# The first two batches loaded by halves of their heads, and a new order of the first steps

## The chip, the cores and the metric

One core of one Trainium2 chip runs one launch of the program. The metric is device time in microseconds (us), the median of the runs shown; the profile comes from one more execution.

## The reference: what is computed

Four batches of 8 heads, 576 positions and 64 columns go through linear attention; its output, as 2304 rows of 512, goes through a mixture of four experts and then through a gated unit:

```python
q_s = exp(q - max(q, axis=-1));  q_s /= sum(q_s, axis=-1) + 1e-9      # softmax over the 64 columns
k_s = exp(k - max(k, axis=2));   k_s /= sum(k_s, axis=2) + 1e-9       # softmax over the 576 positions
kv  = einsum('bhsd,bhde->...', k_s, v)       # 64 x 64 for each head
x   = (q_s @ kv) as [2304, 512]
p   = domain_probs / (domain_probs.sum(-1) + 1e-9)
y   = sum over e of p[:, e] * (relu(x @ w1[e]) @ w2[e])               # 4 experts, 512 -> 1024 -> 512
g   = y @ w_gate;  val = y @ w_val;  out = (silu(g) * val) @ w_out    # 512 -> 1536 -> 512
```

All numbers are float32 (the three weights of the last unit are stored as 64-bit numbers and are decoded on the chip).

## The kernel before, in words

**Precision and products.** Each float32 operand of a matmul is split in a high part (a cast, on ScalarE) and a low part (the difference, on VectorE or GpSimd; both in `split`, L103-105), and each product is made of three matmuls (`mm3`, L107-111). Big products are made with seven products in place of eight, for which sums and differences of the blocks of x and of the weights are needed. `combine_x` (L372-388) makes those of x: four sums (L381-384), and the high and low parts of the seven terms; `combine_acc` (L392) calls it for the tokens that lie in SBUF. The tokens are taken in two halves of two batches; each half is cut in two parts, X and Y, and each part in two groups j of the 512 columns.

**Attention.** A batch has four groups g of two heads. `att_kv` (in the chains below: K) takes the maxima of k over the positions: VectorE's first maxima m (L194), transposes on TensorE (ktp, L198-199), a reduction mx (L202), and a matmul that broadcasts it (kmb, L205); then VectorE's subtraction e (L210, the last 64 positions L213), ScalarE's exponential (L216, L217), the kv product of five matmuls on TensorE (kvp, L221 and L225), and its scaling kk by the reciprocal of the sums rs (L234-239). `att_q` (Q) takes the maxima of q over the columns (L254, L255), subtracts them (L257, L258), takes exponentials (L261, L262), sums (L276, L277), reciprocals (L282, L283) and scales by them on GpSimd (L284, L285); one group of batch 0 takes its sums with the exponentials (qs). `att_x` (X) transposes q on TensorE (qtp, L303, L307), splits it (qT) and multiplies it with kk into x, which ScalarE copies out (L322, L324).

**The first steps.** The first two batches are loaded by `load_batch` (L884-917), all on SyncE's queue: batch 0's k lands in `acc[X]` (acc_67 in the order below), its q in `acc[Y]` (acc_68), v in the tiles vb_82 (heads 0 to 3) and vb_83 (heads 4 to 7); the last 64 positions of k, q and v lie in `rest` (rest_84). Batch 1 lies in the tiles called stage. The work on the two batches, on the first two units of weights and on the first two steps of the experts is cut in pieces by Python generators, and a string of names (L997) says in which order the pieces are written: K01 is the next piece of group 1 of batch 0's k, Q and X likewise (X010: batch 0, group 1, half 0), L and l load weights, A, B, O and o prepare them, P the probabilities, N and M finish x, C0 and C1 combine X's two groups, D0 and D1 Y's, S is a piece of the experts' steps. From that string a scheduler decides what stands on each engine; an engine works its row off in order and waits for semaphores of the others. From the third step on, the order is written out and the change does not touch it.

Of the kernel before, what the change touches and what calls it, by code (L numbers as in the profile page):

```python
# [27 lines left out]
def attention_experts_swiglu(ctx: ExitStack, tc: tile.TileContext, q, k, v, probs, w1, w2, wg, wv, wo, out):  # L28
# [12 lines left out]
    nc = tc.nc  # L41
    B, H, S, D = q.shape
# [329 lines left out]
    def combine_x(b, j, x0, x1, eng):  # L372


        n = N[b]
        h, l = xh[b][:, :, j, :], xl[b][:, :, j, :]
        x0, x1 = (x.rearrange("p (s n) -> p s n", s=2) for x in (x0, x1))
        low = nc.gpsimd
        split(h[:, 0], l[:, 0], x0[:, 0], low)
        split(h[:, 1:3], l[:, 1:3], x1, nc.vector)  # L380
        eng.tensor_tensor(x0[:, 1], x0[:, 1], x0[:, 0], ALU.subtract)  # L381
        eng.tensor_tensor(x1[:, 1], x1[:, 1], x0[:, 1], ALU.subtract)
        eng.tensor_tensor(x0[:, 0], x1[:, 1], x0[:, 0], ALU.subtract)
        eng.tensor_tensor(x1[:, 0], x1[:, 0], x1[:, 1], ALU.subtract)
        yield
        split(h[:, 3:5], l[:, 3:5], x0, low)
        split(h[:, 5:7], l[:, 5:7], x1, nc.vector)
        yield

    parts = {}  # L390

    def combine_acc(b, j, eng=None):  # L392
        if (b, j) not in parts:
            parts[b, j] = combine_x(b, j, accT[b][:, 2 * j, :], accT[b][:, 2 * j + 1, :], eng or nc.vector)
            next(parts[b, j])
        else:
            next(parts.pop((b, j)))
# [386 lines left out]
    if True:  # L784
# [100 lines left out]
        def load_batch(b, kb, qb, vb, rest):  # L885
            kr = rest[:, 0:H * D].rearrange("p (h d) -> p h d", h=H)
            vr = rest[:, H * D:].rearrange("p (h d) -> p h d", h=H)
            for z in range(2):
                h = slice(z * H // 2, (z + 1) * H // 2)
                nc.sync.dma_start(kb[:, h], k[b, h, 0:SM, :].rearrange("h (p c) d -> p h c d", c=C))  # L890
                if z == 0:
                    nc.sync.dma_start(kr[R], k[b, :, SM:S, :].rearrange("h r d -> r h d"))
            for z in range(2):
                h = slice(z * H // 2, (z + 1) * H // 2)
# [102 lines left out]
        for c in '''K01 K01 K00 K00 K02 K01 K00 K03 K00 K03 K01 K01 K03 K03 K00 Q01 Q00 K01 K00 Q01 K02 K02 K02 K03 Q03 Q03 Q01 K03 K01 X010 Q00 K02 Q00 Q02 Q02 X010 K00 K03 X000 X011 X011 A X001 K02 K02 Q03 X001 X011 X030 X000 X000 X031 L K13 X001 X031 Q02 X020 K13 X020 K12 X021 X000 X030 K12 K13 K12 X021 P X020 X010 K11 A K11 X020 K10 O K13 K10 K11 K13 K10 K10 X021 K12 O Q13 K10 Q10 B K13 X011 K12 Q12 Q12 K10 X010 K11 K11 Q11 Q10 Q13 Q10 Q11 K12 K10 Q13 X031 X100 X100 X100 K11 X101 X101 X001 X021 Q12 l X030 K12 K13 X120 X131 K11 X101 N X031 X131 o X121 X120 X120 X120 X121 B X121 C0 X030 Q11 X121 X110 X111 C1 X130 X111 X110 X110 X131 X100 X110 X130 C1 X111 C0 S S X130 S S X131 X130 X111 X101 S S S M S D1 S S S S S S S S D1 S o D0 D0 S'''.split():  # L997
            next(chains[c], None)
# [40 lines left out]
```

## Time and profile before

| what | value |
|---|---|
| median of 3 runs | 1319.56 us (1317.67 to 1324.06) |
| profiled execution: its own time | 1323.6 us |
| profiled execution: span | 1321.8 us |
| mean granted TensorE clock | 0.991 |
| TensorE (PE) busy | 1279.2 us, 97% |
| VectorE (DVE) busy | 946.7 us, 72% |
| ScalarE (ACT) busy | 617.4 us, 47% |
| GpSimd (POOL) busy | 559.7 us, 42% |

The span runs from the first to the last instruction that the profiler saw, the execution's own time some 2 us longer. TensorE's weight loads (PEld) lie beside its matmuls. A busy share is an average over the whole span; the first 90 us, in which the first two batches' attention is done, look different from the rest.

### The profile page before, as it was taken

To read this page: it belongs to the slowest core of one execution; us is meant where nothing else is said; L and a number is where in the kernel's file an instruction comes from. 1 tells how busy PE (TensorE), PEld (TensorE's weight loads), DVE (VectorE), ACT (ScalarE), POOL (GpSimd) and SP (SyncE) were. 2 spreads that over 40 slices of the span, in tenths; PEclk is the share of its full clock that TensorE was granted. 3 is DMA by queue.
4 is the path that set the end of the run, shared out by engine and by line. 5 is a ranking of instruction groups with operands and counts; after the bars stand their busy time and mean duration, and the time that the engine had idled before them with its cause. 6 is when DMAs were issued, how large, how long until landed. Compare 5 with 4: busy or idle time off the path is not lost.

```text
span 1321.8 us, 20267 instructions
## 1 busy us (share of the span) xinstructions
PE 1279.2 (97%) x7568; PEld 1146.3 (87%) x7568; DVE 946.7 (72%) x1584; ACT 617.4 (47%) x1352; POOL 559.7 (42%) x585
## 2 busy tenths in 40 slices
PE   5799999999999998999999999999999899999998
PEld 4578888888888887888988988898998899999997
DVE  6786778877878777778788676656666776666665
ACT  4653445444544454454454444355454444444442
POOL 4543533443353353536445353254344444443320
PEclk9889999999999999999999999999999999999999
DMA  9321433433333333344444332562125567111102
GB/s 211 85 55 40 125 111 92 132 101 111 103 122 105 119 119 102 116 128 135 152 157 128 127 96 81 167 220 88 43 70 164 167 210 241 45 45 49 49 1 72
DMA packets 111298, 148.15 MB, mean 112 GB/s; under 512 B 30560, under 2 KB 71520, under 8 KB 111200
## 3 DMA queue, kind: packets, MB, share of 16 engines
q1 hardware_dynamic: 111200, 146.87, 35.8%
q8 instruction: 59, 0.97, 0.3%
q14 instruction: 39, 0.32, 0.1%
HBM read 109.09 MB, written 37.75 MB: 111 GB/s over the span
## 4 chain that ended last, share of the span: by engine, by line
PE 85%; DVE 6%; POOL 2%; ACT 2%; DMA 2%; issue 1%; SPq 1%; POOLq 0%; ACTq 0%; DVEq 0%
PE o L694 13%; PE o L696 13%; PE o L695 12%; PE h L109 8%; PE h L110 8%; PE h L111 8%; PE h_1g L109 2%; PE h_1g L110 2%; PE h_1g L111 2%; PE h_1v L109 2%; PE h_1v L110 2%; PE h_1v L111 2%; PE kvp L221 1%; PE h_0v L109 1%; PE h_0v L111 1%
## 5 line engine op out<-in xcount | busy, mean ns | idle before, releaser
L694 PE MATMUL o<-oh,hh 128*128 128x512 f32 x792 | 315.1, 398 | 1.8 <-ACT xt L408 1.1
L696 PE MATMUL o<-oh,hl 128*128 128x512 f32 x792 | 313.5, 396 | 2.9 <-DVE hl L644 2.8
L695 PE MATMUL o<-ol,hh 128*128 128x512 f32 x792 | 312.1, 394 | 0.0
L705 DVE SCALAR_TENSOR_TENSOR acc<-o,pn,acc 128x512 f32<-128x512 f32 x270 | 200.1, 743 | 74.7 <-PE o L696 73.9
L504 ACT COPY sn<-h 128x256 f32<-128x256 f32 (+1 forms) x192 | 76.4, 398 | 257.4 <-PE h L111 256.8
L696 PEld LDWEIGHTS o<-oh,hl 128*128 128x128 f32 x792 | 148.6, 188 | 39.5 <-DVE hl L644 4.2
L694 PEld LDWEIGHTS o<-oh,hh 128*128 128x128 f32 x792 | 149.0, 188 | 20.9 <-ACT xt L408 1.6
L639 ACT ACTIVATE hh<-g 128x512 fp32r<-128x512 f32 (+1 forms) x176 | 119.2, 685 | 95.8 <-DVE g L525 42.0
L695 PEld LDWEIGHTS o<-ol,hh 128*128 128x128 f32 x792 | 148.9, 188 | 17.3
L644 DVE SCALAR_TENSOR_TENSOR hl<-g,hh 128x512 fp32r<-128x512 f32 (+1 forms) x128 | 118.1, 925 | 32.3 <-ACT hh L639 29.8
L709 DVE TENSOR_TENSOR acc<-o,acc 128x512 f32<-128x512 f32 x90 | 61.9, 687 | 45.5 <-PE o L696 44.5
L522 ACT COPY g<-h 128x256 f32<-128x256 f32 (+1 forms) x64 | 25.6, 399 | 83.3 <-PE h L111 83.1
L646 DVE TENSOR_TENSOR hl<-g,hh 128x512 fp32r<-128x512 f32 (+1 forms) x48 | 48.0, 999 | 4.0 <-ACT hh L639 3.2
L525 DVE TENSOR_TENSOR g<-h,sn 128x256 f32<-128x256 f32 (+1 forms) x64 | 28.9, 452 | 27.5 <-PE h L111 27.1
L519 DVE TENSOR_TENSOR g<-h,sn 128x256 f32<-128x256 f32 (+1 forms) x64 | 29.0, 453 | 19.4 <-ACT sn L504 19.1
L663 ACT ACTIVATE g<-g 128x512 f32<-128x512 f32 (+1 forms) x48 | 33.0, 688 | 19.9 <-DVE g L525 19.9
L105 POOL TENSOR_TENSOR xo<-xp,xo 128x256 fp32r<-128x256 f32 (+1 forms) x24 | 22.2, 926 | 44.2 <-ACT xo L104 43.4
L504 ACT COPY sn_1g<-h_1g 128x320 f32<-128x320 f32 x36 | 15.4, 426 | 52.0 <-PE h_1g L111 51.8
L565 DVE SCALAR_TENSOR_TENSOR r<-r 128x512 int32<-128x512 int32 x36 | 32.6, 907 | 0.4
L567 DVE CUSTOM_DVE_ANT_0 r<-r 128x1024 uint16<-128x1024 uint16 x36 | 31.4, 873 | 0.3
L675 DVE TENSOR_TENSOR g<-g,v 128x512 f32<-128x512 f32 (+1 forms) x24 | 22.8, 950 | 10.4 <-ACT v L522 10.3
L104 ACT CAST xo<-xp 128x256 fp32r<-128x256 f32 (+1 forms) x56 | 24.2, 433 | 12.9 <-DMA xp<-sd 5.9
(1176 smaller groups left out, 3846.7 us busy)
## 6 DMA issues: line engine op xcount, KB each, us to landing
pd<-xo SPq DMA_DIRECT2D x28, 320.0 KB, 3.2
pd<-xo SPq DMA_DIRECT2D x28, 256.0 KB, 2.6
r<-in_moe_w_gate_dram SPq DMA_DIRECT2D x12, 512.0 KB, 4.1
r<-in_moe_w_val_dram SPq DMA_DIRECT2D x12, 512.0 KB, 4.1
r<-in_moe_w_out_dram SPq DMA_DIRECT2D x12, 512.0 KB, 3.8
xl<-pd SPq DMA_DIRECT2D x14, 320.0 KB, 5.5
xh<-pd SPq DMA_DIRECT2D x14, 320.0 KB, 5.1
out_dram<-acc SPq DMA_DIRECT2D x16, 256.0 KB, 2.4
```

The costliest lines, as they stand in the source:

```text
L109: nc.tensor.matmul(o, wh, xh, start=first, stop=False, skip_group_check=more)
L110: nc.tensor.matmul(o, wh, xl, start=False, stop=False, skip_group_check=more)
L111: nc.tensor.matmul(o, wl, xh, start=False, stop=last, skip_group_check=more)
L504: nc.scalar.copy(sn[z], banks[0])
L639: nc.scalar.activation(hh[:, :, t * n:(t + 1) * n], g[:, :, t], AF.Relu if kind == "e" else AF.Copy)
L644: nc.vector.scalar_tensor_tensor(hl[:, :, ts], g[:, :, t], 0.0, f32(hh[:, :, ts]), ALU.max, ALU.subtract)
L646: nc.vector.tensor_tensor(hl[:, :, ts], g[:, :, t], f32(hh[:, :, ts]), ALU.subtract)
L694: nc.tensor.matmul(p, hh[:, z, ts], w[z][0], start=z == 0, stop=False)
L695: nc.tensor.matmul(p, hh[:, z, ts], w[z][1], start=False, stop=False)
L696: nc.tensor.matmul(p, hl[:, z, ts], w[z][0], start=False, stop=z == NF - 1)
L705: nc.vector.scalar_tensor_tensor(o, p, weight, o, ALU.mult, ALU.add)
L709: nc.vector.tensor_tensor(o, p, o, ALU.add)
```

## The change

Three things change. First, `load_batch` issues its transfers by halves of the heads: for the first four heads k, the remainder of k, q, the remainder of q, and v, and then k, q and v of the other four. Before, both halves of k came first, then both of q, then v of all heads. The transfers themselves are the same, and so are their number and size. Second, the four sums of `combine_x` for X's first group go to GpSimd in place of VectorE (`XENG`), and the low parts are dealt out anew (`XLOW`, four for each part and group; before they alternated between GpSimd and VectorE). Third, the string that orders the pieces of the first steps is another. All line numbers behind the edit shift by one (the sums of `combine_x` are L380-383 then).

```diff
-    def combine_x(b, j, x0, x1, eng):
+    def combine_x(b, j, x0, x1, eng, lows=(nc.gpsimd, nc.vector, nc.gpsimd, nc.vector)):
...
-        low = nc.gpsimd
-        split(h[:, 0], l[:, 0], x0[:, 0], low)
-        split(h[:, 1:3], l[:, 1:3], x1, nc.vector)
+        split(h[:, 0], l[:, 0], x0[:, 0], lows[0])
+        split(h[:, 1:3], l[:, 1:3], x1, lows[1])
         eng.tensor_tensor(x0[:, 1], x0[:, 1], x0[:, 0], ALU.subtract)
...
-        split(h[:, 3:5], l[:, 3:5], x0, low)
-        split(h[:, 5:7], l[:, 5:7], x1, nc.vector)
+        split(h[:, 3:5], l[:, 3:5], x0, lows[2])
+        split(h[:, 5:7], l[:, 5:7], x1, lows[3])
...
-
-    def combine_acc(b, j, eng=None):
+    XENG = [nc.gpsimd, nc.vector, nc.vector, nc.vector]
+    XLOW = [nc.gpsimd, nc.gpsimd, nc.vector, nc.gpsimd, nc.gpsimd, nc.vector, nc.vector, nc.vector, nc.gpsimd, nc.vector, nc.vector, nc.vector, nc.gpsimd, nc.vector, nc.vector, nc.vector]
+
+    def combine_acc(b, j):
...
-            parts[b, j] = combine_x(b, j, accT[b][:, 2 * j, :], accT[b][:, 2 * j + 1, :], eng or nc.vector)
+            parts[b, j] = combine_x(b, j, accT[b][:, 2 * j, :], accT[b][:, 2 * j + 1, :], XENG[2 * b + j], XLOW[8 * b + 4 * j:8 * b + 4 * j + 4])
...
             for z in range(2):
+                nc.gpsimd.memset(vb[z][:, :, :, D:], 1.0)
+            nc.gpsimd.memset(vr[R, :, D:], 1.0)
+            for z in range(2):
                 h = slice(z * H // 2, (z + 1) * H // 2)
                 nc.sync.dma_start(kb[:, h], k[b, h, 0:SM, :].rearrange("h (p c) d -> p h c d", c=C))
                 if z == 0:
                     nc.sync.dma_start(kr[R], k[b, :, SM:S, :].rearrange("h r d -> r h d"))
-            for z in range(2):
-                h = slice(z * H // 2, (z + 1) * H // 2)
                 nc.sync.dma_start(qb[:, h], q[b, h, 0:SM, :].rearrange("h (p c) d -> p h c d", c=C))
                 if z == 0:
                     nc.sync.dma_start(kr[RQ], q[b, :, SM:S, :].rearrange("h r d -> r h d"))
-            for z in range(2):
-                nc.gpsimd.memset(vb[z][:, :, :, D:], 1.0)
-            nc.gpsimd.memset(vr[R, :, D:], 1.0)
-            for h in range(H):
-                nc.sync.dma_start(
-                    vb[h // 4][:, :, h % 4, 0:D], v[b, h, 0:SM, :].rearrange("(p c) d -> p c d", c=C)
-                )
-                if h == 1:
-                    nc.sync.dma_start(vr[R, :, 0:D], v[b, :, SM:S, :].rearrange("h r d -> r h d"))
+                for x in range(z * H // 2, (z + 1) * H // 2):
+                    nc.sync.dma_start(
+                        vb[z][:, :, x % 4, 0:D], v[b, x, 0:SM, :].rearrange("(p c) d -> p c d", c=C)
+                    )
+                    if x == 1:
+                        nc.sync.dma_start(vr[R, :, 0:D], v[b, :, SM:S, :].rearrange("h r d -> r h d"))
...
```

The string L997 begins `K01 K01 K00 K00 K02 K01 K00 K03` before and `K01 K00 K03 K01 K01 K00 K00 K01` after the change. What it does is seen in the rows that come out of it.

The first place is SyncE's queue at the start of the program. Its rows before the change:

```order
L890 DMA acc_67<-in_k_dram 128x4x256
L892 DMA rest_84<-in_k_dram 64x8x64
L890 DMA acc_67<-in_k_dram 128x4x256
L895 DMA acc_68<-in_q_dram 128x4x256
L897 DMA rest_84<-in_q_dram 64x8x64
L895 DMA acc_68<-in_q_dram 128x4x256
L902 DMA vb_82<-in_v_dram 128x4x64 x2
L906 DMA rest_84<-in_v_dram 64x8x64
L902 DMA vb_82<-in_v_dram 128x4x64 x2
L902 DMA vb_83<-in_v_dram 128x4x64 x4
```

And with the change:

```order
L894 DMA acc_67<-in_k_dram 128x4x256
L896 DMA rest_84<-in_k_dram 64x8x64
L897 DMA acc_68<-in_q_dram 128x4x256
L899 DMA rest_84<-in_q_dram 64x8x64
L901 DMA vb_82<-in_v_dram 128x4x64 x2
L905 DMA rest_84<-in_v_dram 64x8x64
L901 DMA vb_82<-in_v_dram 128x4x64 x2
L894 DMA acc_67<-in_k_dram 128x4x256
L897 DMA acc_68<-in_q_dram 128x4x256
L901 DMA vb_83<-in_v_dram 128x4x64 x4
```

The second half of k (the second row with acc_67) moves from the third place to the tenth transfer, behind the first half of q and v of heads 0 to 3.

The second place is VectorE's row up to the subtraction e_161, on which the first kv product works. Before the change (the maxima m of all four groups lie ahead of these rows):

```order
L210 TENSOR_TENSOR e_207<-acc_67,kmb_168 128x2x4x64
L213 TENSOR_TENSOR rest_84<-rest_84,kmb_168 64x128
L254 TENSOR_REDUCE qm_212<-acc_68 128x2x4
L255 TENSOR_REDUCE qm_212<-rest_84 64x2
L277 TENSOR_REDUCE qm_175<-rest_84 64x2
L210 TENSOR_TENSOR e_256<-acc_67,kmb_205 128x2x4x64
L213 TENSOR_TENSOR rest_84<-rest_84,kmb_205 64x128
L276 TENSOR_REDUCE qm_212<-e_207 128x2x4
L277 TENSOR_REDUCE qm_212<-rest_84 64x2
L282 TENSOR_SCALAR qm_212<-qm_212 128x10
L283 RECIPROCAL qm_212<-qm_212 128x10
L210 TENSOR_TENSOR e_161<-acc_67,kmb_159 128x2x4x64
```

With the change:

```order
L202 TENSOR_REDUCE mx_143<-ktp_139 128x1
L202 TENSOR_REDUCE mx_149<-ktp_145 128x1
L194 TENSOR_TENSOR m_137<-acc_67 128x256
L194 TENSOR_TENSOR m_153<-acc_67 128x256
L202 TENSOR_REDUCE mx_166<-ktp_157 128x1
L254 TENSOR_REDUCE qm_173<-acc_68 128x2x4
L255 TENSOR_REDUCE qm_173<-rest_84 64x2
L254 TENSOR_REDUCE qm_179<-acc_68 128x2x4
L210 TENSOR_TENSOR e_161<-acc_67,kmb_151 128x2x4x64
```

The subtractions of two other groups are no longer ahead of e_161; the maxima m_137 and m_153, which read the second half of k, are.

The third place is TensorE's row with the four kv products of batch 0 (kvp; each has four matmuls L221 and one L225). Before the change:

```order
L205 MATMUL kmb_205<-ident,mx_203 128x128
L221 MATMUL kvp_185<-vb_82,e_161 128x130 x4
L225 MATMUL kvp_185<-rest_84 128x130
L221 MATMUL kvp_191<-vb_82,e_170 128x130 x4
L225 MATMUL kvp_191<-rest_84 128x130
L221 MATMUL kvp_226<-vb_83,e_207 128x130 x4
L225 MATMUL kvp_226<-rest_84 128x130
L303 MATMUL qtp_241<-ident,e_161 128x128 x2
L221 MATMUL kvp_320<-vb_83,e_256 128x130 x4
L225 MATMUL kvp_320<-rest_84 128x130
```

With the change:

```order
L221 MATMUL kvp_183<-vb_82,e_161 128x130 x4
L225 MATMUL kvp_183<-rest_84 128x130
L221 MATMUL kvp_191<-vb_82,e_168 128x130 x4
L225 MATMUL kvp_191<-rest_84 128x130
L303 MATMUL qtp_223<-ident,e_161 128x128 x2
L221 MATMUL kvp_240<-vb_83,e_199 128x130 x4
L225 MATMUL kvp_240<-rest_84 128x130
L205 MATMUL kmb_254<-ident,mx_238 128x128
L303 MATMUL qtp_299<-ident,e_168 128x128 x2
L303 MATMUL qtp_302<-ident,e_168 128x128 x2
L307 MATMUL qtp_302<-ident,rest_84 128x64
L221 MATMUL kvp_341<-vb_83,e_256 128x130 x4
```

The broadcast kmb of the last group's maxima moves from ahead of the first kv product to behind the third, and the fourth product moves behind transposes of q. (A row that transposes another group stands between the last two.)

What waits for that broadcast on VectorE, with the change, are these rows, in order:

```order
L210 TENSOR_TENSOR e_256<-acc_67,kmb_254 128x2x4x64
L213 TENSOR_TENSOR rest_84<-rest_84,kmb_254 64x128
L258 TENSOR_TENSOR rest_84<-rest_84,qm_261 64x128
L234 TENSOR_SCALAR rs_277<-kvp_191 128x1
L234 TENSOR_SCALAR rs_286<-kvp_240 128x1
L282 TENSOR_SCALAR qs_226<-qs_226 128x10
L235 RECIPROCAL rs_277<-rs_277 128x1
L235 RECIPROCAL rs_286<-rs_286 128x1
L283 RECIPROCAL qs_226<-qs_226 128x10
```

The reciprocal qs_226 at the end is what GpSimd scales e_168 by; the transposes qtp_299 and qtp_302 read the result.

The fourth place is GpSimd's row where batch 1's q begins (the tile stage, L257; ol and wl1a are low parts of weights). Before the change:

```order
L257 TENSOR_TENSOR e_456<-stage_114,qm_475 128x2x4x64
L258 TENSOR_TENSOR stage_114<-stage_114,qm_475 64x128
L257 TENSOR_TENSOR e_481<-stage_114,qm_486 128x2x4x64
L258 TENSOR_TENSOR stage_114<-stage_114,qm_486 64x128
L257 TENSOR_TENSOR stage_114<-stage_114,qm_514 128x2x4x64
L258 TENSOR_TENSOR stage_114<-stage_114,qm_514 64x128
L105 TENSOR_TENSOR ol_445<-raw0o,oh_444 128x512
L105 TENSOR_TENSOR wl1a<-raw1a,wh1a 128x512
L105 TENSOR_TENSOR wl1a<-raw1a,wh1a 128x256
```

With the change:

```order
L380 TENSOR_TENSOR acc_67<-acc_67 128x256
L381 TENSOR_TENSOR acc_67<-acc_67 128x256
L105 TENSOR_TENSOR xl_685<-acc_67,xh_684 128x256
L383 TENSOR_TENSOR acc_67<-acc_67 128x256
L382 TENSOR_TENSOR acc_67<-acc_67 128x256
L105 TENSOR_TENSOR xl_685<-acc_67,xh_684 128x2x256
L105 TENSOR_TENSOR xl_685<-acc_67,xh_684 128x256
L105 TENSOR_TENSOR ol_448<-raw0o,oh_447 128x512
L253 MEMSET qm_475 64x2
L253 MEMSET qm_501 64x2
L253 MEMSET qm_521 64x2
L105 TENSOR_TENSOR wl1a<-raw1a,wh1a 128x512
```

Four sums and the low parts of x and of weights come ahead of batch 1's first subtraction L257 now; that follows three rows later.

From TensorE's row that begins unit 1's third stage on (a matmul L109 into h with the weights wh1a, at 90.49 us in the trace before), the rows of both programs agree on every engine but for numbers in names.

## Rows read from the trace of the kernel before

**Rows 1.** The page: TensorE's line (busy us, share, instructions).

```profile
PE 1279.2 (97%) x7568; PEld 1146.3 (87%) x7568; DVE 946.7 (72%) x1584; ACT 617.4 (47%) x1352; POOL 559.7 (42%) x585
```

**Rows 2.** Windows view: busy us by engine, granted clock, DMA share, GB/s.

```profile
core 0: us, PE busy (x) PEld busy (x) DVE busy (x) ACT busy (x) POOL busy (x), PEclk, DMA share, GB/s
0.00:19.35 19.35, 6.02 (x20) 3.75 (x21) 10.81 (x28) 4.86 (x10) 5.62 (x26) 1.00 0.93 211
19.35:48.40 29.05, 27.38 (x100) 21.77 (x101) 18.59 (x55) 17.96 (x61) 14.84 (x20) 1.00 0.75 178
48.40:59.40 11.00, 6.31 (x39) 5.15 (x39) 10.65 (x24) 8.70 (x22) 8.12 (x13) 0.97 0.00 1
59.40:79.10 19.70, 14.72 (x56) 11.99 (x56) 15.84 (x47) 10.57 (x27) 15.56 (x18) 0.50 0.19 54
79.10:90.49 11.39, 11.39 (x75) 9.81 (x74) 8.07 (x17) 7.72 (x19) 2.21 (x6) 0.99 0.41 110
```

**Rows 3.** Timeline of TensorE (start us, us, line, tiles; idle before and releaser).

```profile
43.51 0.41 PE L109 MATMUL h<-xh,wh0a 128*128 128x256 f32 x1
...
59.05 2.10 PE L221 MATMUL kvp<-stage,e 128*128 128x130 f32 x8 [3.11 <-ACT e L216]
...
90.49 0.28 PE L109 MATMUL h<-xh,wh1a 128*128 128x256 f32 x1
```

**Rows 4.** Timeline of VectorE and TensorE around the first kv products.

```profile
18.01 0.63 DVE L210 TENSOR_TENSOR e<-acc,kmb 128x512 f32<-128x512 f32 x1
18.55 0.27 DVE L213 TENSOR_TENSOR rest<-rest,kmb 64x128 f32<-64x128 f32 x1
...
19.35 2.10 PE L221 MATMUL kvp<-vb,e 128*128 128x130 f32 x8 [5.20 <-DMA pt<-in_moe_domain_probs_dram]
...
22.11 2.10 PE L221 MATMUL kvp<-vb,e 128*128 128x130 f32 x8
```

**Rows 5.** Timeline of the first 10 us: VectorE's maxima and SyncE's queue.

```profile
5.12 0.76 DVE L194 TENSOR_TENSOR m<-acc 128x256 f32<-128x256 f32 x2 [5.12 <-DMA acc<-in_k_dram]
5.64 2.63 SPq L902 DMA_DIRECT2D vb<-in_v_dram  x2
...
8.30 0.76 DVE L194 TENSOR_TENSOR m<-acc 128x256 f32<-128x256 f32 x2 [2.41 <-DMA acc<-in_k_dram]
```

**Rows 6.** Transfers issued at 5.64 (KB, us from issue to landing).

```profile
vb<-in_v_dram SPq DMA_DIRECT2D x1, 128.0 KB, 7.9
```

**Rows 7.** Timeline of the first 19 us, VectorE and TensorE.

```profile
10.54 0.68 DVE L254 TENSOR_REDUCE qm<-acc 128x8 f32<-128x512 f32 x1
...
11.47 0.63 PE L198 MATMUL ktp<-ident,m 128*128 128x128 f32 x2
...
12.81 0.49 DVE L202 TENSOR_REDUCE mx<-ktp 128x1 f32<-128x320 f32 x1
```

**Rows 8.** Timeline up to the first x, VectorE, GpSimd and TensorE.

```profile
30.90 0.20 DVE L283 RECIPROCAL qs<-qs 128x10 f32<-128x10 f32 x1
...
31.25 1.04 POOL L284 TENSOR_TENSOR e<-e,qs 128x512 f32<-128x512 f32 x1 [2.62 <-DVE rs L235]
...
32.34 1.11 PE L303 MATMUL qtp<-ident,e 128*128 128x128 f32 x4 [1.56 <-POOL e L284]
...
35.03 0.58 PE L109 MATMUL x<-qT010h,kk 128*128 128x256 f32 x1
```

**Rows 9.** Timeline of batch 1, GpSimd and TensorE.

```profile
50.81 1.05 POOL L257 TENSOR_TENSOR e<-stage,qm 128x512 f32<-128x512 f32 x1 [1.08 <-DVE qm L254]
...
70.64 0.66 PE L303 MATMUL qtp<-ident,e 128*128 128x128 f32 x2 [1.77 <-DVE kk L239]
```

**Rows 10.** GpSimd in batch 1: the windows view (columns as in rows 2).

```profile
50.81:74.55 23.74, 14.25 (x62) 11.46 (x63) 19.96 (x57) 14.94 (x39) 21.07 (x24) 0.67 0.15 44
```

**Rows 11.** Timeline of GpSimd: a low part and a sum.

```profile
56.81 1.28 POOL L105 TENSOR_TENSOR ol<-raw0o,oh 128x512 fp32r<-128x512 f32 x1 [0.82 <-POOL stage L258]
...
61.34 0.73 POOL L479 TENSOR_TENSOR raw1a<-raw1a 128x256 f32<-128x256 f32 x1
```

More of the change, by code (lines that the diff above doesn't have):

```diff
@@ L996, in attention_experts_swiglu @@
                     chains[f"X{b}{g}{z}"] = att_x(b, g, z, xb, b == 0)
-        for c in '''K01 K01 K00 K00 K02 K01 K00 K03 K00 K03 K01 K01 K03 K03 K00 Q01 Q00 K01 K00 Q01 K02 K02 K02 K03 Q03 Q03 Q01 K03 K01 X010 Q00 K02 Q00 Q02 Q02 X010 K00 K03 X000 X011 X011 A X001 K02 K02 Q03 X001 X011 X030 X000 X000 X031 L K13 X001 X031 Q02 X020 K13 X020 K12 X021 X000 X030 K12 K13 K12 X021 P X020 X010 K11 A K11 X020 K10 O K13 K10 K11 K13 K10 K10 X021 K12 O Q13 K10 Q10 B K13 X011 K12 Q12 Q12 K10 X010 K11 K11 Q11 Q10 Q13 Q10 Q11 K12 K10 Q13 X031 X100 X100 X100 K11 X101 X101 X001 X021 Q12 l X030 K12 K13 X120 X131 K11 X101 N X031 X131 o X121 X120 X120 X120 X121 B X121 C0 X030 Q11 X121 X110 X111 C1 X130 X111 X110 X110 X131 X100 X110 X130 C1 X111 C0 S S X130 S S X131 X130 X111 X101 S S S M S D1 S S S S S S S S D1 S o D0 D0 S'''.split():
+        for c in '''K01 K00 K03 K01 K01 K00 K00 K01 K02 K00 K03 K01 K03 K00 Q01 Q00 K01 K03 K00 Q01 K03 Q01 K02 K01 X010 Q00 K02 K03 Q03 Q03 K02 K02 Q02 X011 Q02 X010 K00 K03 Q00 X000 X001 X011 Q03 A X011 X030 L X001 K02 X001 X031 Q02 K02 K13 X000 X000 X031 X020 K13 K12 X021 X000 X030 X020 K12 K13 K12 P X020 K10 K12 K13 K10 A K10 X010 X021 O X020 K13 K11 K11 K10 X021 K11 O Q13 K12 K10 X010 K10 Q13 K11 Q10 Q10 K13 K12 Q12 Q12 K10 X011 K11 Q11 Q10 Q13 X001 Q11 X031 B X100 K11 X101 X101 Q12 X030 K12 l X021 K13 X100 X100 X120 X120 X131 K11 X031 X131 o X121 X120 X120 X121 B X100 X101 N X121 C0 Q11 X121 X110 X111 X030 C1 X111 X130 X110 X130 C1 C0 X110 X130 S S S S S X111 X111 X101 X131 S S S X110 X130 S X131 S M S D1 S S D0 S S S o S S D1 D0'''.split():
             next(chains[c], None)
```

## The prediction

> **What bounds the kernel now.** The page first: TensorE is busy for 97% of the span [rows 1]. An edit that saves work elsewhere therefore gains only where TensorE waits, so I cut the span into stages [rows 2]. In the first 19.35 us TensorE is busy for 6.02 us and the transfers run at 211 GB/s; from 19.35 to 48.40 it is busy for 27.38 of 29.05; from 48.40 to 79.10 for 21.03 of 30.70; from there on it hardly waits (11.39 of 11.39). All that this change can touch is the first 90 us. What sets their end is TensorE's row order: from the row at 90.49 on [rows 3] both programs have the same matmuls in the same order. The question is how much sooner or later that row starts.
>
> The clock is part of it. The profile's clock column reads 1.00 in the second stage, but the same pass of 256 columns takes 0.41 us at 43.51 and 0.28 at 90.49 [rows 3]: there it is still the 1.2 GHz level, until about 48.4. Then the 2.4 GHz level holds up to 59.4, the granted clock is 0.50 for 19.70 us (1.2 GHz), and from 79.1 on it is 2.4 GHz for good [rows 2]. Just before the fall TensorE had waited for 3.11 us at once [rows 3].
>
> **The first kv product.** It starts at 19.35 [rows 4], on the exponential of e, which VectorE's subtraction released at 18.01. VectorE, not a transfer, set this: in the row order before, that subtraction stands behind those of two other groups.
>
> The new order of loads moves k's second half from third to tenth place. It lands when k's and q's first halves, their remainders, v0, v1, v's remainder, v2 and v3 have: with itself 3 x 512 + 7 x 128 = 2432 KB. Before, just as many had landed with v0 (four halves, two remainders, v0): issued at 5.64 [rows 5] and 7.9 us under way [rows 6], so at 13.5. By another row, 640 KB land between the first and the second k half, 5.12 to 8.30 [rows 5], and at that pace the 1920 KB behind the first half take 9.5 us: 14.7. So T, the landing of k's second half, is 13.5 to 14.7; I take 14.0, between rows that are equally near. That it lands at 8.3, as now, is rival B.
>
> What waits for T is the point. In VectorE's new order the two maxima m of the second half stand ahead of the subtraction that releases the first kv product, with one reduction of mx and three of q behind them. VectorE is in order, so it has nothing from about 9 until T. From T: 0.4 for m (0.76 for two) [rows 5], 0.9 for the transposes (0.63 for two, and a short third), 0.5 for mx, then 0.68, a short one of 0.27 and 0.68 again [rows 4, 7] = 3.5. The subtraction starts at 17.5 (17.0 to 18.2) against 18.01, and the first kv product at 18.85. The earlier loads gain 0.5 us at this place (between a loss of 0.2 and a gain of 1.0), and no more, because the first group's work now waits behind the half that was pushed back.
>
> The Trainium skill, "DMA: Bandwidth & Descriptors" (section Specifications), gives 435 GB/s as the ceiling of the 16 engines. By that figure alone T would be an estimated 8.3 us: 5.12 less 512 KB at 211 GB/s is a start at 2.6, and 2432 KB take 5.7 from there; the time would be that of rival B. The trace shows 211 GB/s with the engines at 0.93 [rows 2], not 435, so the measurement decides.
>
> **The middle, to the first x.** In the new order TensorE has two kv products (2.76 us each with the remainder, 19.35 to 22.11 [rows 4]), a transpose pair, the third product, and only then the broadcast of the last group's maxima (kmb), which before stood ahead of the first product. VectorE's subtraction for the fourth group waits for that broadcast, and behind it in VectorE's queue are the remainder, q's remainder, and six short ones (0.20 for the like, half of it overlapped), whose last is the reciprocal that releases GpSimd's scaling of e: 0.63 + 2 x 0.27 + 6 x 0.11 = 1.85 us [rows 4, 8]. GpSimd's scaling takes 1.04 [rows 8]. TensorE's next row needs it: idle for 1.85 + 1.04 + 0.1 = 3.0 us, where the wait for the same scaling was 1.56 before [rows 8]. Then two transpose sets, the fourth product, a third set, and a cast with its low part (0.9, by two operations on 128 x 320 like the mx of 0.49 [rows 7]), which before was done in the wait. From the first product to the first x: 4 x 2.76 of products, 3.7 of transposes, 0.5 of kmb, 3.0 and 0.9 of waits = 19.1 us, against 15.7 before (19.35 to 35.03) [rows 4, 8]. With the 0.5 gained the first x is at 38.0, +2.9. Of these some 1.0 is work only drawn ahead of it (kmb, a transpose set); the idle time added is 3.9 - 1.6 = 2.3, less 0.5 gained: +1.8 for TensorE. Bounds: +0.4 if the broadcast's chain is through early and the wait stays at 1.6; +2.5 with T at 14.7.
>
> **Batch 1.** From 50.81 to 74.55, its last scaling of batch 1, GpSimd is the engine with the least air: 21.07 us of 23.74 [rows 9, 10]. What comes before on ScalarE, the exponentials of e, waits for TensorE's maxima of batch 1, which follow the first x; with the 1.8 added they come at about 52. In GpSimd's new order the low parts of the w_out unit and of the next weights stand ahead of q's subtractions, so the exponentials of q wait for casts that ScalarE makes later. I put GpSimd's start at 53.5 and its end at 53.5 + 21.07 + 1.8 of waits = 76.4 against 74.55: +1.9. The transposes of q that before waited to 70.64 [rows 9] have then a kv product ahead of them and come at 73.4: +2.8. From there to the row at 90.49 TensorE has the same work as before and little air. I carry 2.5, between 1.9 and 2.8.
>
> **Sums and low parts.** X's first half gives its four sums to GpSimd: 4 x 0.73 = 2.9 us there, by a sum of the same shape [rows 11]; VectorE is rid of them. Of the low parts, some go each way: X's second half and both of Y put more on VectorE. None of the sums' results is needed before the weave, where TensorE is the bound; VectorE is busy for 15.84 of 19.70 in the fourth stage [rows 2] and this cover is what hides them. If GpSimd is the bound of batch 1 instead, its 2.9 us count (rival D). Two of the sums lie before batch 1's start, and I price this part at nothing.
>
> **Sum.** +2.5 at the row at 90.49, and nothing behind it: 1323.6 + 2.5 = 1326.1 for the profiled execution; its own time is 4.0 above the median of the runs shown, so 1319.56 + 2.5 = 1322.1. A difference of 0.5% (6.6 us) is about what a measurement tells from no change. Own range: from +0.4 (the wait at the first x stays at 1.6 and batch 1 adds nothing) to +4.7 (2.8 with T's late end, 0.7, and GpSimd's sums of 1.2 beyond their cover), on a median that itself lies between 1317.67 and 1324.06: 1318 to 1326.
>
> **Rivals.**
> A, above: chance 0.50.
> B, the second k half lands early, at 8.3 as now, because queued transfers share the engines. Then nothing holds VectorE, the subtraction starts at about 12, the first kv product at 13.2, 6 us early. For it speaks the room in the first stage, where TensorE is idle for 19.35 - 6.02 = 13.3 us [rows 2]; against it, that now the halves land in the order of issue, 3.18 us apart [rows 5]. The idle 2.3 us of the middle and 0.7 at batch 1 stay: 1319.56 - 6 + 3.0 = 1316.6. Break-even is where the start gains 3.0, at T = 11.5. Chance 0.12.
> C, the clock. If TensorE's waits between 55 and 65 shrink, the 2.4 GHz level may hold through the fourth stage. It had 14.72 us busy there at 0.50 [rows 2]; at double the clock 7.4 are saved: 1319.56 + 2.5 - 7.4 = 1314.7, and 1312 where the first rise comes earlier as well. For it: one kv product is moved off the stage. Against it: waits of 3 us remain by the order. Chance 0.16.
> D, GpSimd becomes the bound. The 2.9 us of sums and one 1.28 us low part that stand ahead of batch 1 delay all of its 21 us: +2.5 + 4.2 = 1326.3 (the low part at 56.81 [rows 11]). For it: GpSimd's small air [rows 10]. It decides from the point at which GpSimd's last scaling ends after 77.5. Chance 0.22.
>
> **Numbers.** The likeliest is A's 1322.1. Faster by over 0.5% (under 1313): the part of C with both rises early, and some of B with the whole 6 us kept, 0.10. Slower by over 0.5% (over 1326.2): half of D, and 0.09 of A and the rest where waits of 1 to 2 us add up behind the later first x, 0.20. Within: 0.70. The range 1313 to 1329 takes in T's bounds, B and most of C and D, and leaves out C's lower and D's upper end.
>
> **What will show it.** Right: VectorE's second pair of m waits on k's transfer until 13.5 to 14.7; the first kv product at 18.3 to 19.5; a wait of about 3 us on GpSimd's scaling behind the third; the first x at 37 to 39; batch 1's last scaling near 76; the row at 90.49 now at 93. Wrong: the second half's k before 11.5 (B), a granted clock of 1.00 between 60 and 79 (C), sums of x on GpSimd next to a TensorE wait (D), or any difference behind the common row, which I exclude: same order, same tiles.

## The result and the profile after

The change made the kernel slower by about half a per cent: 1326.51 us (1325.45 to 1327.35, 7 runs) against 1319.56 us (1315.61 to 1324.30, 7 runs), ratio 1.0055, 95% interval [1.0034, 1.0075]. In the two profiled executions the difference is smaller, 1323.8 against 1321.8 us of span. Most of what follows is about these two numbers, +7.0 and +2.0.

The head of the page of the changed kernel (compare [rows 1]):

```profile
span 1323.8 us, 20275 instructions
PE 1276.9 (96%) x7568; PEld 1145.0 (86%) x7568; DVE 945.1 (71%) x1582; ACT 616.9 (47%) x1352; POOL 558.1 (42%) x587
```

The start of the changed kernel in the timeline of VectorE, TensorE and GpSimd, which answers to [rows 4, 5, 8] (start us, us, engine, line, tiles, idle time before with its releaser):

```profile
14.24 0.76 DVE L194 TENSOR_TENSOR m<-acc 128x256 f32<-128x256 f32 x2 [5.99 <-DMA acc<-in_k_dram]
17.78 0.68 DVE L210 TENSOR_TENSOR e<-acc,kmb 128x512 f32<-128x512 f32 x1
...
19.17 2.10 PE L221 MATMUL kvp<-vb,e 128*128 128x130 f32 x8 [1.83 <-ACT e L216]
...
24.46 1.07 PE L221 MATMUL kvp<-vb,e 128*128 128x130 f32 x8
...
25.88 0.49 PE L205 MATMUL kmb<-ident,mx 128*128 128x128 f32 x2
28.61 1.04 POOL L284 TENSOR_TENSOR e<-e,qs 128x512 f32<-128x512 f32 x1 [0.62 <-DVE qs L283]
29.71 0.69 PE L303 MATMUL qtp<-ident,e 128*128 128x128 f32 x4 [3.35 <-POOL e L284]
...
31.31 0.69 PE L303 MATMUL qtp<-ident,e 128*128 128x128 f32 x2 [0.62 <-POOL e L284]
31.79 1.94 PE L221 MATMUL kvp<-vb,e 128*128 128x130 f32 x8
...
36.41 0.64 PE L109 MATMUL x<-qT011h,kk 128*128 128x320 f32 x1 [1.04 <-DVE qT011l L105]
...
92.80 0.28 PE L109 MATMUL h<-xh,wh1a 128*128 128x256 f32 x1
```

What the reader sees: the second half of k lands at 14.24, VectorE has waited 5.99 us for it, the first kv product starts at 19.17 (19.35 before), and behind the third product and kmb TensorE waits 3.35 us for GpSimd. The third product takes 1.07 us and the fourth 1.94: between them the clock has gone from its 2.4 GHz level back to 1.2 GHz. The row that both programs have in common (called the common row from here on) stands at 92.80 in place of 90.49: +2.3, and 1231.0 us follow it, against 1231.3 before.

### The profile page after: what moved, and what is told of

Same layout as the page of the kernel before. It is cut to its first block, busy times and chain, and to the rows that moved or that the text cites. A ratio compares the mean times of both kernels' runs of the same rounds, so it can differ in the third digit from the quotient of the medians.

```text
span 1323.8 us, 20275 instructions
## 1 busy us (share of the span) xinstructions
PE 1276.9 (96%) x7568; PEld 1145.0 (86%) x7568; DVE 945.1 (71%) x1582; ACT 616.9 (47%) x1352; POOL 558.1 (42%) x587
## 4 chain that ended last, share of the span: by engine, by line
PE 86%; DVE 5%; POOL 2%; ACT 2%; DMA 2%; issue 1%; SPq 1%; POOLq 0%; ACTq 0%; DVEq 0%
PE o L695 13%; PE o L697 13%; PE o L696 13%; PE h L109 9%; PE h L110 8%; PE h L111 8%; PE h_1g L109 2%; PE h_1g L111 2%; PE h_1g L110 2%; PE h_1v L109 2%; PE h_1v L111 2%; PE h_1v L110 2%; PE h_0v L109 1%; PE h_0v L111 1%; PE h_0v L110 1%
## 5 line engine op out<-in xcount | busy, mean ns | idle before, releaser
L697 PEld LDWEIGHTS o<-oh,hl 128*128 128x128 f32 x792 | 148.9, 188 | 39.2 <-DVE hl L645 3.8
L526 DVE TENSOR_TENSOR g<-h,sn 128x256 f32<-128x256 f32 (+1 forms) x64 | 28.9, 452 | 27.4 <-PE h L111 27.1
L520 DVE TENSOR_TENSOR g<-h,sn 128x256 f32<-128x256 f32 (+1 forms) x64 | 29.0, 453 | 18.0 <-ACT sn L505 17.6
L511 DVE TENSOR_TENSOR g<-h,sn 128x256 f32<-128x256 f32 (+1 forms) x64 | 28.8, 450 | 1.4 <-PE h L111 0.9
```

The lines of the kernel that those rows point to most:

```text
L697: nc.tensor.matmul(p, hl[:, z, ts], w[z][0], start=False, stop=z == NF - 1)
```

## The experiments

Twelve kernels ran. The times "of the kernel before" beside them are 1317.5 to 1318.0 (medians of 11 to 18 runs). The ratios and their 95% intervals are estimated from all runs and differ a little from the quotients of the medians.

**The kernel before once more (e1).** No edit.

> The kernel before, unchanged, as its own control. Theory W (the change costs 2 to 3 us of waits; what the median shows beyond that, 7 us against 2.0 in the two profiles, comes from executions of the kernel before that run part of the first 90 us at the higher of TensorE's two clock levels): 1315 to 1324, and if the profiled execution is below 1320, its granted clock between 59 and 79 us is above 0.6 and the matmul into h that stood at 90.49 comes earlier by just that difference. Rival V (executions vary behind the first 100 us): the same range, but that matmul stays at 90.5 and the difference arises later.

1318.01 us (1315.16 to 1323.29, 12 runs), ratio 0.9999 [0.9985, 1.0014]. Its profiled execution has a span of 1316.8, and the common row is at 84.03, 6.46 us earlier than in the trace that the prediction read. The windows view is cut at the first kv product, the first x, GpSimd's first subtraction of batch 1, the end of its last scaling, and the common row. First come the second, third and fifth stage in the trace of before; the fourth is [rows 10]. The stage's length is the first number behind the stretch, and the clock column is the third from the right:

```profile
19.35:35.03 15.68, 14.12 (x53) 11.31 (x53) 10.64 (x33) 10.58 (x39) 11.57 (x15) 1.00 0.97 212
35.03:50.81 15.78, 15.49 (x62) 12.22 (x61) 10.33 (x27) 8.47 (x25) 4.60 (x10) 1.00 0.42 118
74.55:90.49 15.94, 15.94 (x93) 13.74 (x92) 12.22 (x25) 10.97 (x27) 3.49 (x7) 0.85 0.30 80
```

Then e1, all five stages, and last a stretch that its clock marks off:

```profile
0.00:19.27 19.27, 5.95 (x21) 3.76 (x21) 10.91 (x28) 4.87 (x10) 5.60 (x26) 1.00 0.94 205
19.27:31.89 12.62, 10.45 (x52) 8.31 (x53) 10.63 (x33) 10.46 (x39) 11.13 (x15) 0.93 0.87 215
31.89:45.20 13.31, 12.47 (x62) 9.68 (x61) 10.57 (x27) 8.80 (x26) 5.00 (x10) 0.81 0.86 194
45.20:68.90 23.70, 13.79 (x62) 10.99 (x63) 19.93 (x57) 14.66 (x38) 21.01 (x24) 0.68 0.14 44
68.90:84.03 15.13, 14.96 (x93) 12.70 (x92) 12.13 (x25) 10.87 (x27) 3.48 (x7) 0.93 0.30 84
30.05:36.88 6.83, 6.72 (x25) 5.12 (x24) 3.89 (x10) 4.29 (x14) 3.91 (x4) 0.50 1.30 221
```

The same rows of the same program: the second and third stage take 12.62 and 13.31 in place of 15.68 and 15.78, and TensorE's busy time in them falls from 14.12 and 15.49 to 10.45 and 12.47. It is faster there, not less loaded. The clock column reads 1.00 until a first change is seen, so there the durations tell the level: the third kv product takes 2.10 us in the trace of before, as the two ahead of it do [rows 4], and 1.16 in e1. Before:

```profile
24.87 2.10 PE L221 MATMUL kvp<-vb,e 128*128 128x130 f32 x8
```

e1:

```profile
24.10 1.16 PE L221 MATMUL kvp<-vb,e 128*128 128x130 f32 x8
...
29.59 0.73 PE L303 MATMUL qtp<-ident,e 128*128 128x128 f32 x4 [2.14 <-POOL e L284]
...
84.03 0.28 PE L109 MATMUL h<-xh,wh1a 128*128 128x256 f32 x1
```

So in e1 the 2.4 GHz level comes during the second product, some 25 us before it came in the trace of before (48.4). It falls to 1.2 GHz at 30.05, just behind a wait of 2.14 us, and is back at 36.88, while TensorE hardly waits (6.72 of 6.83 us busy).

Of theory W's statement on the kernel before, the clock holds (0.70 between 59 and 79) and the place holds, before the common row; the row moved by 6.46 us, and not by just the 5.0 us between the two spans. V's does not hold: behind the common row e1 takes 1232.8 us, 1.5 more, not less. The trace read for the prediction was an execution with a late rise, and its own 1323.6 us lie near the upper end of what the kernel before does.

**Each part alone on the kernel before (e2, e3, e4).**

```diff
e2: load_batch with the new order of transfers; combine_x, combine_acc and the string as before
e3: combine_x and combine_acc with XENG and XLOW; load_batch and the string as before
e4: the new string; load_batch, combine_x and combine_acc as before
```

> The kernel before with the new order of transfers alone; the string and the engines of sums and low parts as before. Theory W: k's second half lands at 13.5 to 14.5, VectorE's second pair of maxima waits for it, and the first kv product starts between 18.5 and 19.5; median 1320 to 1323. Theory G (the sums and low parts on GpSimd cost the time): 1319.6, no change. Theory S (the new string costs the time by itself): 1319.6 too.

> The kernel before with the sums and low parts on the new engines alone. Theory W: no change, 1318 to 1321. Theory G: 1323 to 1327, with batch 1's first subtraction on GpSimd 2 to 4 us later than 50.8. Theory S: no change.

> The kernel before with the new string alone; transfers in the old order, engines as before. Theory W: k's second half lands at 8.3 and nothing waits for it, the order of the kv products still puts the last group's broadcast behind the third product: the wait of 3 us there stays, the start gains or stays; 1318 to 1323. Theory S: 1324 to 1327. Theory G: 1319.6.

Measured: e2 1330.38 us, 1.0092 [1.0074, 1.0110]; e3 1325.29 us, 1.0052 [1.0033, 1.0070]; e4 1333.83 us, 1.0115 [1.0095, 1.0135]. Every one of the three expectations of theory W is too low, and none of the theories had all three parts slower: by 12.8, 7.7 and 16.2 us against 1317.63, together 36.6, where the whole change costs 8.9 against the same 1317.63. In e2's profile k's second half lands at 12.82 and the first kv product starts at 18.08, both a little before the times that theory W gave and the latter before the 19.27 and 19.35 of the kernel before, so e2's loss does not arise at the start. e3's time lies in theory G's range, but batch 1's first subtraction is at 52.36, 1.6 us later than 50.81 and not 2 to 4, and e5 below speaks against G.

**Each part undone in the changed kernel (e5, e10, e11).** These complete the table of two by two by two.

```diff
e5:  XENG = [nc.vector] * 4;  XLOW = [nc.gpsimd, nc.vector] * 8   (the old engines)
e10: load_batch as before   (the old transfers)
e11: the string as before
```

> The changed kernel with the sums and low parts of x on their old engines; transfers and string as changed. Theory G (GpSimd's sums and low parts cost the time): back to 1319 to 1321. Theory W (waits behind the late half and between kv products cost it): 1325 to 1328, since the rows up to 45 us are the same and VectorE pays 1.6 us for the sums in place of GpSimd's 2.9. Theory T (the string was fitted to these transfers and these engines as a whole, so that a part of it alone is worse): above 1328.

> The changed kernel with the transfers in the old order; new string and new engines. Theory T (the string fits these transfers and engines as a whole): 1328 to 1335, beside 1333.8 for the string alone. Theory W (the late second half is what costs): k's second half lands at 8.3, no wait of 5.9 us on VectorE, 1318 to 1323.

> The changed kernel with the old string; new transfers and new engines. Theory T: above the changed kernel, 1328 to 1338, since either part alone cost 7.7 and 12.7 on the kernel before. Rival S (the new string is what costs): 1319 to 1324.

| transfers | engines | string | median us | ratio, 95% interval |
|---|---|---|---|---|
| old | old | old | 1317.63 | |
| new | old | old | 1330.38 | 1.0092 [1.0074, 1.0110] |
| old | new | old | 1325.29 | 1.0052 [1.0033, 1.0070] |
| old | old | new | 1333.83 | 1.0115 [1.0095, 1.0135] |
| new | old | new | 1332.40 | 1.0111 [1.0092, 1.0129] |
| old | new | new | 1329.94 | 1.0098 [1.0079, 1.0117] |
| new | new | old | 1332.81 | 1.0112 [1.0097, 1.0128] |
| new | new | new | 1326.51 | 1.0055 [1.0034, 1.0075] |

Theory T holds in all three: whatever part is undone, it gets slower, by 5.9, 3.4 and 6.3 us. No price belongs to a part: the engines cost 7.7 in the old order and save 5.9 in the new one. A scheduler makes the rows anew from all three, and e10 shows what that does. There k's second half lands at 8.29 (VectorE waits 2.20 us for it) and the first kv product starts at 16.61, earlier than in the changed kernel; but the first x comes at 38.13, 1.7 us later, and in batch 1 TensorE waits 6.66 us at once for VectorE's kk, where the changed kernel waits 2.12. e10, then the changed kernel:

```profile
75.26 0.66 PE L303 MATMUL qtp<-ident,e 128*128 128x128 f32 x2 [6.66 <-DVE kk L239]
```

```profile
72.54 0.66 PE L303 MATMUL qtp<-ident,e 128*128 128x128 f32 x2 [2.12 <-DVE kk L239]
```

**TensorE's waits filled (e6, e7).** Nothing in the row order changes, on any engine; transposes of the identity are put into TensorE's longest waits. Their results are unused. The output is not the reference's, most likely because those put in during batch 1 write to the bank of h and destroy partial sums there.

```diff
+def _fill(nc, where):
...
+        at = rows.index(of(name)[-1]) + 1
+        for _ in range(count):
+            nc.tensor.transpose(free, ident, ident)
+            rows.insert(at, end.pop())
...
e6: where = kmb00 20, kmb02 18, kvp10 30, kvp11 12 (on the changed kernel)
e7: where = kmb02 18, kvp02 12, kmb11 18, kvp11 22, kvp12 10 (on the kernel before)
```

> The changed kernel with its row order unchanged on every engine, and 80 transposes of the identity put into TensorE's four longest waits of the first 75 us (20 at 9 us, 18 at 26, 30 at 59, 12 at 70), results unused. Theory K (a wait costs a second time, because TensorE's clock falls behind it and stays low): the granted clock stays at 1.00 from about 20 us to 80 but for at most one short stretch, the matmul into h that stands at 92.8 comes at 84 to 88, median 1317 to 1322. Rival N (the waits alone matter, TensorE's speed does not since others are late): the clock rises but that matmul stays within 1.5 us of 92.8, median 1325 to 1328. Rival O (the transposes overrun the waits and come on top): later than 93, above 1328.

> The kernel before with its row order unchanged and 80 transposes of the identity put into TensorE's five longest waits behind 14 us, results unused. Theory K: clock 1.00 through the first 80 us nearly without a break, the matmul into h comes at 80 to 85 in place of 87.5 to 90.5, median 1310 to 1315, and less scatter between executions than 1315 to 1324. Rival N: within 1.5 us of 1318. Rival O: above 1320.

e7: 1318.69 us (1316.59 to 1320.26, 12 runs), 1.0001 [0.9991, 1.0011]. Its windows, from the first kv product on, by the same cuts:

```profile
19.25:31.30 12.05, 9.51 (x64) 7.61 (x65) 10.34 (x32) 10.47 (x39) 10.56 (x14) 1.00 0.89 221
31.30:43.42 12.12, 10.69 (x62) 7.97 (x61) 11.12 (x29) 8.71 (x26) 5.60 (x11) 1.00 0.87 207
43.42:67.75 24.33, 18.10 (x117) 15.35 (x118) 21.72 (x60) 16.61 (x42) 21.66 (x24) 0.93 0.15 44
67.75:82.77 15.02, 14.46 (x88) 12.62 (x87) 10.92 (x23) 9.09 (x22) 3.50 (x8) 0.89 0.31 85
```

With the clock up, the stages up to batch 1 take 12.05 and 12.12: the level alone moves them, as e1 suggested. The common row comes at 82.77, where theory K put it, but the median does not go down: K's 1310 to 1315 is refuted, and rival N's 1318 within 1.5 us holds. The fourth stage takes 24.33 us with the clock at 0.93, 23.70 in e1 at 0.68 and 23.74 in the trace of before at 0.67, so TensorE's clock does not set its length; GpSimd is busy for 21.66 us of it. Behind the common row e7 takes 1234.0 us, against 1232.8 in e1, so the row's 1.3 us are not seen at the end of this execution. The scatter shrank as expected, from 8.1 us to 3.7.

e6: 1327.09 us (1325.45 to 1328.32, 6 runs), 1.0065 [1.0051, 1.0080]. First the windows of the changed kernel and one stretch that its clock marks off, then the windows of e6:

```profile
19.17:36.41 17.24, 12.24 (x54) 9.67 (x54) 13.79 (x47) 13.52 (x46) 11.85 (x15) 0.82 1.05 215
36.41:55.87 19.46, 18.16 (x77) 14.64 (x78) 12.30 (x28) 12.38 (x35) 14.85 (x19) 0.63 0.24 76
55.87:75.42 19.55, 9.13 (x40) 6.91 (x39) 14.25 (x47) 10.36 (x26) 16.21 (x22) 0.63 0.18 53
75.42:92.80 17.38, 17.06 (x100) 15.35 (x101) 13.89 (x31) 11.63 (x28) 2.21 (x7) 0.83 0.27 73
30.21:47.27 17.06, 15.27 (x58) 11.84 (x57) 8.55 (x25) 9.56 (x29) 14.75 (x18) 0.50 0.70 187
```

```profile
18.32:37.24 18.92, 15.77 (x72) 13.29 (x72) 13.84 (x47) 13.08 (x46) 11.35 (x15) 0.68 1.04 225
37.24:57.08 19.84, 18.31 (x78) 14.15 (x78) 13.53 (x31) 12.71 (x36) 15.34 (x20) 0.66 0.22 69
57.08:76.66 19.58, 12.57 (x79) 10.64 (x79) 13.17 (x44) 10.38 (x26) 16.23 (x22) 0.86 0.09 33
76.66:93.43 16.77, 16.45 (x100) 14.74 (x100) 13.88 (x31) 11.65 (x28) 2.22 (x7) 0.86 0.27 76
```

The row stays at 93.43 and the median in N's range. In the fourth stage the clock is 0.86 in place of 0.63 and its length is 19.58 in place of 19.55: there rival N is shown. For the second and third stage the fill did not raise the clock as a whole (0.68 and 0.66), so they are not tested by it.

**The subtractions of the first half first (e8).** The maxima of k's second half go behind them in the string, and VectorE's order of the first 16 pieces is that of the string.

```diff
-K01 K00 K03 K01 K01 K00 K00 K01 K02 K00 K03 K01 K03 K00 Q01 Q00 K01 K03 K00 Q01 K03 Q01 K02 K01 X010 Q00 K02 K03
+K01 K00 K01 K01 K00 K00 K01 K00 K01 K00 Q01 Q00 K01 K03 K02 K03 K03 K00 Q01 K03 Q01 K03 K02 K01 X010 Q00 K02 K03
+        with tc.manual_schedule(engines={mybir.EngineType.DVE}):
+            for c in first:
+                next(chains[c], None)
```

> The changed kernel with the maxima of k's second half moved behind the subtractions of the first half: VectorE's order of the first 16 pieces is written out, so that the first two subtractions stand ahead of the wait for the second half. What follows is scheduled anew. Theory W: the first kv product starts at 11.5 to 13 in place of 19.2 (v0 and v1 have landed then), the first x 2 to 4 us earlier, median 1321 to 1325. Rival T (only the whole order counts, the start is absorbed by the next wait): first kv product early, but first x within 1 us of 36.4 and 1326 or more.

1334.28 us, 1.0120 [1.0102, 1.0138], the slowest of all. TensorE's timeline:

```profile
12.31 2.07 PE L221 MATMUL kvp<-vb,e 128*128 128x130 f32 x8 [3.10 <-DMA vb<-in_v_dram]
...
25.31 0.69 PE L303 MATMUL qtp<-ident,e 128*128 128x128 f32 x2 [5.20 <-POOL e L284]
...
34.12 1.11 PE L303 MATMUL qtp<-ident,e 128*128 128x128 f32 x4 [4.25 <-POOL e L284]
...
39.83 0.62 PE L109 MATMUL x<-qT011h,kk 128*128 128x320 f32 x1
```

The first kv product comes at 12.31, 6.9 us early, and the first x at 39.83, 3.4 us late: what the start gains is given to two waits for GpSimd's scaling. Theory W's reason for the size (the late half costs the time at the start) falls with it, as far as a newly scheduled rest allows. Rival T's "1326 or more" holds; its first x within 1 us of 36.4 does not.

**Batch 1's q ahead of the weights (e9).**

```diff
-K10 A K10 X010 X021 O X020 K13 K11 K11 K10 X021 K11 O Q13 K12 K10 X010 K10 Q13 K11 Q10 Q10 K13 K12 Q12 Q12 K10
+K10 K10 X010 X021 X020 K13 K11 K11 K10 X021 K11 Q13 K12 K10 X010 K10 Q10 A Q13 O K11 Q10 K13 K12 Q12 O Q12 K10
```

> The changed kernel with batch 1's first pieces of q written ahead of the preparation of weights in the string; TensorE's order is the same but for names, GpSimd's moves batch 1's subtractions ahead of one low part and two sums of weights. Theory P (GpSimd's and ScalarE's chain of batch 1 sets the row at 92.8, so that what stands ahead of its subtractions is paid in full): the second subtraction starts 1 to 3 us before 60.9, the last scaling before 74.0, the row at 90 to 92, median 1323 to 1325.5. Rival C (the clock level decides): row within 1 us of 92.8 unless the granted clock between 60 and 81 changes.

1325.46 us (1323.67 to 1326.68, 6 runs), 1.0052 [1.0038, 1.0066]: no difference from the changed kernel that can be told. In its profile the second subtraction starts 23.2 us behind the first x (61.64 and 38.40), against 24.5 in the changed kernel (60.88 and 36.41), and the last operation of the last scaling 39.2 behind it (77.55), against 38.6 (74.96): the subtractions came forward and the low part that was moved behind them was paid there. Theory P is not borne out. The common row is at 95.28 in this execution; the clock between 60 and 81 differs (0.58, against 0.52 in the changed kernel), so rival C is not tested.

**The changed kernel once more (e12).** No edit.

> The changed kernel, unchanged, as control: 1325 to 1328. If its scatter is small because its first 45 us are bound by VectorE and GpSimd and not by TensorE, the first x stands within 1 us of 36.4 and the row within 1.5 us of 92.8 whatever the clock does; if it is only luck of the one profile, they move by several us, as between the two profiles of the kernel before (first x 35.0 and 31.9, row 90.5 and 84.0).

1325.46 us (1324.86 to 1327.38, 3 runs), 1.0057 [1.0037, 1.0076]. First x at 35.84, row at 92.31: 0.6 and 0.5 us earlier than in the first profile, as the first kv product is (18.59). The stages agree to 0.1 us (17.25, 19.53, 19.56, 17.38), though the clock in the third is 0.71 in place of 0.63. Up to 47 us the two profiles have the same levels, so their agreement there does not show what another level would do; e9 does, below.

## Why the prediction was right or wrong

The measured 1326.51 us lie in the range of 1313 to 1329, and the forecast of a small loss was right; its size for the median was not, 7.0 in place of 2.5 us. The time is above A's own range of 1318 to 1326 (whose upper end does not follow from its terms: 1319.56 + 4.7 is 1324.3, and 1324.06 + 4.7 is 1328.8), and it falls, by 0.3 us, in the class "slower by over 0.5%", which had a chance of 0.20.

**The start: right.** T was put at 14.0 (13.5 to 14.7), measured 14.24; the subtraction at 17.5, measured 17.78; the first kv product at 18.85, measured 19.17. That 2432 KB, k's second half among them, have to land first, at the rate of the rows, is what set it. Rival B is out.

**The middle: the mechanism right.** The wait for GpSimd behind the third product was put at 3.0 and is 3.35, the wait for the cast at 0.9 and is 1.04. The chain that the prediction named does release it, but it is not alone: GpSimd had been idle for only 0.62 us before that scaling, so by an estimate from this row TensorE would have waited some 2.8 us without it. The first x was put at 38.0 and came at 36.41, since TensorE ran part of this stage at the 2.4 GHz level, which the sum had not assumed. In e9, with the same rows up to there and the level up only at 36 us, it came at 38.40.

**Batch 1 and the common row: the number near, by luck.** GpSimd's start was put at 53.5 and came at 55.87, its end at 76.4 and came at 75.42; the row at 93.0, measured 92.80. Between start and end the sum carried the 21.07 us that GpSimd works there before the change, though it had put part of that work ahead of the start; 16.21 were left. From the end to the row it carried 16.6 us, and 17.38 were measured. So the three terms are off by +2.4, -3.3 and +0.8 us, and these cancel. Against the profiled execution of before the sum was to give +2.5 and the row gives +2.3, and this is luck too. TensorE has the same 286 matmuls up to the row in both programs; its busy time up to it (first number behind the length) in the trace of before, in e1 and in the changed kernel:

```profile
0.00:90.48 90.48, 65.80 (x286) 52.47 (x287) 63.95 (x166) 49.80 (x137) 46.34 (x81) 0.89 0.53 128
0.00:84.02 84.02, 57.61 (x286) 45.44 (x287) 64.16 (x166) 49.65 (x137) 46.23 (x81) 0.86 0.58 138
0.00:92.79 92.79, 62.44 (x286) 49.94 (x287) 60.10 (x163) 49.84 (x137) 48.41 (x85) 0.78 0.54 125
```

TensorE is idle for 24.7, 26.4 and 30.4 us of these. Against the trace of before the changed kernel has 5.7 us more idle time, and not 2.5; that the row moved by only 2.3 comes from 3.4 us less busy time at the higher level, which the sum did not assume. (A part of the idle time is the higher level's own: e1 has 1.7 us more of it than the trace of before, on the same rows.) Against e1 it has 3.9 us more idle and 4.8 us more busy time. (e12 has 29.3 idle; e2, e3, e4, e5, e10 and e11 have 29.7 to 34.7.)

**The step that failed** is the one in the paragraph on the sum: "its own time is 4.0 above the median of the runs shown, so 1319.56 + 2.5". It takes a difference that holds against one execution and adds it to the median of others. The 4.0 us were not an offset that both kernels share. They are the late rise of the clock in that one execution (e1, whose own 1318.61 us are near the median, has the row 6.46 us earlier). Both profiles of the changed kernel have the early rise, and yet stand 1.8 to 2.3 us behind a kernel before that had the late one: an early rise is worth less to it. The idle time added, put at some 2.5, was mis-sized as well, as the rows above show. Set against e1, stage by stage, the changed kernel's +8.8 us at the common row are -0.1 up to the first kv product, +4.6 up to the first x, +6.2 up to batch 1 on GpSimd, -4.2 in batch 1 and +2.3 behind it (92.80 - 84.03 = 8.77).

1.8 us are given back behind the row, where e1 takes 1232.8 and the changed kernel 1231.0 us. Some 0.7 of them arise in e1 between 501 and 504.5 us, where its granted clock is 0.50 and that of the changed kernel 1.00; the rest comes in steps of 0.3 to 0.4 us. So the clock is not at 2.4 GHz "for good" behind 79 us, as the prediction read it: the granted clock falls to 0.50 for some 3.4 us near 1000 us in the trace of before, near 1000 and 1040 in the changed kernel, and near 500, 1000 and 1030 in e1.

Why an early rise is worth less: in the kernel before the second and third stage are TensorE's (14.12 of 15.68 and 15.49 of 15.78 us busy in the trace of before), so they shrink with the clock, to 12.62 and 13.31 in e1 and 12.05 and 12.12 in e7. In the changed kernel the 2.4 GHz level is there at the third product as well (1.07 us), but from 26.4 TensorE waits 3.35, 0.62 and 1.04 us for GpSimd and VectorE, which the level does not shorten (3.21, 0.19 and 1.30 in e9, at 1.2 GHz up to 36 us). Its second stage, 17.24 and 17.25 in its two profiles, is 18.9 in e9, which has the same rows there and a late rise (its first three kv products take 2.10, 2.10 and 1.94 us): 1.7 us from the clock, and a little more if e9's last 2.4 us there were not at 2.4 GHz too, where the kernel before gets 3.1. This much is shown, for the second stage.

The level is also lost for longer. In e1 and in the changed kernel it comes at 23 us and falls at 30, behind the wait for GpSimd; e1 has it back at 36.88, the changed kernel at 47.27 (0.50 from 30.21 on). So most of the changed kernel's third stage runs at 1.2 GHz, with TensorE busy for 18.16 of 19.46 us, on 77 matmuls in place of 62. Whether the missing clock or GpSimd's load there (14.85 us busy against 4.60 and 5.00 in the two traces of before) makes the third stage's 19.46 us is not shown: both profiles of the changed kernel are at 1.2 GHz up to 47 us, e6 did not raise the level there, and e9, which tried to lighten GpSimd's load, moved too little to tell.

**The price of the parts.** "I price this part at nothing", of the sums and low parts, and the 0.5 us gained by the loads are not borne out: alone they cost 7.7 and 12.8 us, and in the changed kernel they save 5.9 and 3.4. The two prices were read from rows whose order the parts themselves change. The sum over the order that comes out, walked through row by row, was near up to the first x.

**Rivals.** C was wrong way round: the clock does decide some 6 us, but in the kernel before. D's 1326.3 is the time nearest to the measured one, but D (GpSimd the bound in batch 1 by its sums) is not what happened: its stage in batch 1 got shorter, 19.55 against 23.74, as its work went ahead of it, its last scaling ended at 75.42 and not after 77.5, and with the sums back on VectorE (e5) the kernel is slower still. What stays open: why the rise comes at some 23 us in one execution of the kernel before and at 48 in another, with the same rows up to there and the first kv products at 19.27 and 19.35; why the level is back 10 us later in the changed kernel than in e1; and what of the third stage is the clock's and what GpSimd's.

No version here beats the kernel before; e7, whose output is not the reference's, equals it.

## What to carry to other kernels

Before a difference read from a trace is added to a median, look whether that one execution is a typical one: take the kernel before a second time and compare the stages, above all where the clock can change. Where two traces are compared, split the way to a common row in busy and idle time: here a row that moved by the forecast 2.3 us hid 5.7 us more idle and 3.4 us less busy time. A stage in which an engine is busy all the time gains from its clock; here the stage with waits for other engines in it gained about half as much, so a change that adds waits also lost part of what the clock would have given. The parts of this change had no price of their own: each cost time alone and saved time beside the other two.

## What the runs showed of the hardware

Two executions of one program had TensorE first at its 2.4 GHz level at 23 and at 48 us, and were 6.46 us apart at the same row, with the same instructions. With the early rise, the level fell again at 30 us in the kernel before and in the changed one, behind waits of 2.14 and 3.35 us; it was back at 36.88 and at 47.27. With TensorE's waits filled it held nearly through (a granted clock of 0.93 and 0.89 in the last two stages before the common row), that row came 1.3 us earlier than in e1, and the executions' scatter fell from 8.1 to 3.7 us, with no better median. The changed kernel's stages from its first kv product on agreed to 0.1 us between its two profiles.
